# Softmax factors by way of DRAM instead of TensorE, and one load per head instead of one per pair

## The chip, the core and the metric

One core of a Trainium2 chip runs the whole program. Its engines each follow their own list of instructions: TensorE (PE, with its weight loads listed as PEld), VectorE (DVE), ScalarE (ACT), GpSimd (POOL) and SyncE (SP, which only issues DMAs). The metric is the device time in microseconds (us) of one execution; lower is better.

## What is computed

Attention with a mask from hashed buckets, and behind it a gated feed-forward layer. Batch 4, 8 heads, 768 positions, head dimension 64, all in float32:

```
mask   = bucket(q) == bucket(k)            # 6 sign bits of q @ proj, k @ proj
scores = where(mask, q @ k.T / 8, -1e9)    # per batch and head, 768 x 768
attn   = exp(scores - max) / (sum + 1e-9)
x      = attn @ v                          # heads side by side: (4, 768, 512)
h      = relu(x @ w_in)                    # (4, 768, 1024)
out    = (h * sigmoid(conv3(h))) @ w_out
```

## The kernel before

Two heads make a **pair**: 4 pairs for each of 4 batches, 16 in all, named `0_0` to `3_3`. A pair is cut into 12 **units** (6 blocks of 128 queries, 2 heads), and the 192 units run in one loop over `i`; `k` is a unit's place in its pair, 0 to 11. Iteration `i` issues, in this order, the scores `s` of unit `i` (L257, PE), its masked maximum (L270, DVE), the transposes `t` of unit `i-3` (L297, PE) and their copy to SBUF `at` (L304, ACT), and the exponential of unit `i` (L277, ACT), which also leaves the sum of each row. Scores and transposes share a ring of three PSUM tiles (tag `S`), so the scores of a unit reuse the tile of the transposes of two units earlier and wait for their copy.

Every fourth iteration (k = 3, 7, 11; in the text a **burst**) has more: the product with the values `v` (L325, PE) of the last finished group of four units (256 queries, both heads), some steps that decode the float64 weights of the feed-forward layer (L91 to L101 on DVE, a cast L110 on ACT, L111 and L112 on POOL), and a load of raw weights (L132, issued by ACT). How many steps a burst issues stands in `AVS`, `RATE` and `PREP_N`; the order on each engine is just the order in which the code issues.

For the first 7 pairs (not `late`) the division by the sum is done after the product with the values. `Unit.reciprocals` (L291, L292) makes `inv`, 128 queries by 4 (2 blocks by 2 heads), one number per query on the partition of that query. The product `v` has head and dimension on the partitions and queries along the row, so the numbers have to be turned and spread. `spread` (L319) does this on PE, ahead of the 12 chunk products: four products of `inv`, broadcast to 64 columns, with the identity matrix, into the second half of the PSUM tile `av`. `factors` (L330, ACT) copies that to `rs`, and `out` (L333, DVE) multiplies. Later pairs are normalised earlier (L285).

While a pair runs, the next one is prepared: `R` holds queries and keys of both heads (768 KB). `hash` (L186, PE, at k = 3) needs both heads. `split` (head 0 at k = 1 and 3, head 1 at k = 5 and 7) makes on POOL the high part `hi` (L171) and in place the low part (L176), and SP sends these to their places in `Q`, `K`, `q`, `k` (L174, L178). The hash bits go through DVE (L189) and POOL (L191, k = 4) and leave in 8 small DMAs on SP (L195). There is one `R` buffer, so the load for the pair after next (L158, at k = 7) waits until the last low parts have been sent.

Behind pairs 6, 10, 14 and 15 stands a feed-forward stage (`ffn`, L368, L398) of one batch, in which steps of the preparation go on.

All DMAs of the program share eight completion counters, `DMAHW0` to `DMAHW7`, which are given out in turn. A DMA waits on its issuing engine until the one eight before it has landed, whichever engine had issued that one.

Of the kernel before, what the change touches and what calls it, by code (L numbers as in the profile page):

```python
# [7 lines left out]
F32 = mybir.dt.float32  # L8
F32R = mybir.dt.float32r
# [8 lines left out]
P = 128  # L18
# [3 lines left out]
QB = 256  # L22
# [11 lines left out]
AVS = (1 + NCK, 0, 0, 0)  # L34
PREP = 1
PREP_N = 6
# [6 lines left out]
def lsh_attention_conv_ffn(ctx, tc, qk, v, hw, w_in, conv_w, w_out, consts, ident_in, out):  # L43
# [4 lines left out]
    ps = ctx.enter_context(tc.tile_pool(name="ps", bufs=2, space=PSUM))  # L48

# [94 lines left out]
    class Pair:  # L144
        def __init__(self, b, p):
            self.b, self.p, self.nm = b, p, f"{b}_{p}"
            self.late = b * NP + p >= LATE
            self.inv = None

        def load(self):  # L150
            nm = self.nm
            self.R = ring(wp, 1, [P, 2, S], F32R, "R", f"R{nm}")
            src = qk[self.b, 2 * self.p:2 * self.p + 2].rearrange("h p s -> p h s")
            if self.b == self.p == 0:
                for h in range(2):
                    nc.sync.dma_start(self.R[:, h].bitcast(F32), src[:, h])
            else:
                nc.sync.dma_start(self.R.bitcast(F32), src)  # L158
# [8 lines left out]
        def split(self, h):  # L167

            lo, R = self.R[:, h], self.R[:, h].bitcast(F32)
# [6 lines left out]
            nc.gpsimd.tensor_tensor(lo, R, hi.bitcast(F32), ALU.subtract)  # L176
            for dst, src in ((self.Q1[64:, h], lo[:64]), (self.K2[:64, h], lo[64:])):
                nc.sync.dma_start(dst.bitcast(F32), src.bitcast(F32))  # L178

        def hash(self):  # L180
            hp = ring(ps, 3, [P, 2, 512], F32, "S", f"hash{self.nm}")
            R = self.R.bitcast(F32)
            for h in range(2):
                for half in range(2):
                    g = 32 * (2 * h + half)
                    nc.tensor.matmul(hp[g:g + 32, 0, :HS], hw_sb[:, :32], R[:, h, half * HS:(half + 1) * HS],  # L186
                                     start=True, stop=True, tile_position=(0, g))
# [22 lines left out]
        def prepare_now(self):  # L210
# [3 lines left out]
            for h in range(2):  # L214
                hps.append(ring(ps, 2, [P, 512], F32, "M", f"hash{nm}_{h}")[:, :HS])
                for g in range(4):
                    c, half = 32 * (1 + g // 2), g % 2
                    nc.tensor.matmul(hps[h][32 * g:32 * g + 32], hw_sb[:, c:c + 32],
                                     self.R[:, h, half * HS:(half + 1) * HS].bitcast(F32),
                                     start=True, stop=True, tile_position=(0, 32 * g))  # L220
            for h in range(2):
                R = self.R[:, h].bitcast(F32)
# [22 lines left out]
    class Unit:  # L245
# [14 lines left out]
        def maximum(self, prev):  # L260
# [6 lines left out]
            self.sum = self.st[:, 2:3] if pr.late else pr.sums[:, 2 * self.tq + self.h, 0:1]  # L267
# [25 lines left out]

        def transposes(self):
# [12 lines left out]
    def values(pr, qb, ats, inv):  # L307
# [7 lines left out]
        def spread():  # L315

            for t in range(QB // P):
                for h in range(2):
                    nc.tensor.matmul(av[h * D:(h + 1) * D, QB + t * P:QB + (t + 1) * P],  # L319
                                     inv[:, 2 * t + h:2 * t + h + 1].to_broadcast([P, D]), ident,  # L320
                                     start=True, stop=True, tile_position=(0, h * D))

# [5 lines left out]

        def factors():
            nc.scalar.copy(rs, av[:, QB:2 * QB])  # L330
# [18 lines left out]
        rs = ring(wp, 2, [P, QB], F32, "rs", f"rs{pr.nm}_{qb}")  # L349
        return [spread, *chunks], (factors, out, parts)  # L350
# [91 lines left out]
    pairs[0].load()  # L442
# [6 lines left out]
    pairs[1].load()  # L449
    av, outs, lows, early = [], [], [], None  # L450
    n = len(units)
    ffn_after = {min((b + 1) * NP - 1 + DEFER, B * NP - 1): b for b in range(B)}
    for i in range(n + LAG):
# [22 lines left out]
        if two and not two.pair.late and two.tq == QB // P - 1 and two.h == 1:  # L476
            two.reciprocals()
# [20 lines left out]
        for _ in range(1 + NCK if ending else AVS[(i - LAG) % 4]):  # L498
# [20 lines left out]
        if w and w.tq == QB // P - 1 and w.h == 1:  # L519
            if not ending:  # L520
                av.append(values(w.pair, w.qb, w.pair.at, w.pair.inv))
            else:
                def fill():
                    steps, last = values(w.pair, w.qb, w.pair.at, w.pair.inv)
# [56 lines left out]
```

## Time and profile before

| | |
|---|---|
| time, median of 3 runs | 740.08 us (740.05 to 745.73) |
| profiled execution | 739.48 us, its span 737.5 us |
| granted TensorE clock | 0.997 |
| busy: PE, DVE, ACT, POOL | 710.9, 487.3, 498.5, 331.9 us |
| attention of the first 7 pairs | about 0 to 221 us of the span |
| L319 (`spread`) on PE, L330 (`factors`) on ACT | 13.8 us in 168 instructions, 7.8 us in 21 |

The span runs from the first to the last instruction; the execution has 1.98 us around it. A busy time joins overlapping instructions, since matrix products are pipelined: from start to start the next one often comes sooner than the listed length.

### The profile page before, as it was taken

The page shows a single profiled execution, that of the slowest core. Times are in us where ns is not written, and L with a number is a line of the kernel's source. Part 1 is how long each engine was busy: PE and PEld are TensorE (multiplying, and loading weights), DVE is VectorE, ACT ScalarE, POOL GpSimd, SP SyncE. Part 2 cuts the span into 40 slices and gives each one's busy share as a digit, 9 for nine tenths or more (in the row PEclk, how much of TensorE's full clock was granted, in tenths as well). Part 3 has the DMA queues.
Part 4 walks back from the last instruction along what each step waited for, and adds up shares of the span by engine and source line. Part 5 has one row for each costly group of instructions (what it writes and reads, how often), then busy time and mean ns, then how long its engine had stood idle before and what let it go on. Part 6 is the DMA issues. An engine that isn't in the chain of part 4 may idle for free.

```text
span 737.5 us, 13543 instructions
## 1 busy us (share of the span) xinstructions
PE 710.9 (96%) x4720; PEld 589.0 (80%) x4720; DVE 487.3 (66%) x1211; ACT 498.5 (68%) x937; POOL 331.9 (45%) x334
## 2 busy tenths in 40 slices
PE   6998999899899999999999999999999999999997
PEld 3787777678778988777877998778778899878996
DVE  7977878788775755666665666466666566555663
ACT  5788578678684554877877554778778655585554
POOL 4265456357463522475673532355755232241321
PEclk9999999999999999999999999999999999999999
DMA  4867666663552310237545130324463001100011
GB/s 143 222 187 202 165 186 166 165 166 89 147 146 52 86 44 36 72 77 189 139 105 149 34 94 3 108 60 113 117 180 95 1 0 44 44 1 1 0 44 43
DMA packets 30355, 72.17 MB, mean 98 GB/s; under 512 B 5936, under 2 KB 7504, under 8 KB 30288
## 3 DMA queue, kind: packets, MB, share of 16 engines
q1 hardware_dynamic: 27696, 62.88, 32.0%
q10 hardware_dynamic: 2592, 8.44, 3.3%
q8 instruction: 37, 0.61, 0.3%
q14 instruction: 30, 0.25, 0.1%
HBM read 27.40 MB, written 6.29 MB: 46 GB/s over the span
## 4 chain that ended last, share of the span: by engine, by line
PE 69%; DMA 11%; POOL 7%; issue 5%; DVE 4%; SPq 3%; ACT 1%; POOLq 0%; DVEq 0%; ACTq 0%
PE h L368 19%; PE o L398 18%; PE v L325 11%; PE s L257 10%; PE t L297 9%; DMA R<-in_qk 6%; DMA k<-R 4%; POOL R L176 2%; SPq L174 2%; DVE e L270 1%; DMA K<-hi 1%; PE hash L186 1%; POOL hi L171 1%; ACT e L277 1%; SPq L178 1%
## 5 line engine op out<-in xcount | busy, mean ns | idle before, releaser
L270 DVE TENSOR_SCALAR_CACHE_REDUCE e<-s 128x768 f32<-128x768 f32 x192 | 183.2, 954 | 81.2 <-PE s L257 70.6
L277 ACT ACTIVATE e<-e,st 128x768 f32<-128x768 f32 x192 | 181.3, 944 | 10.3 <-DVE st L284 5.0
L304 ACT COPY at<-t 128x768 f32<-128x768 f32 x192 | 152.3, 794 | 47.0 <-PE t L297 47.0
L297 PE MATMUL t<-ident,e 128*128 128x128 f32 x1152 | 160.0, 275 | 3.6 <-POOL e L285 1.5
L377 DVE SCALAR_TENSOR_TENSOR ht<-ht,cw 128x384 f32<-128x384 f32 (+1 forms) x128 | 114.7, 896 | 71.2 <-ACT ht L375 69.0
L387 POOL TENSOR_TENSOR g<-ht,g 128x384 fp32r<-128x384 f32 x64 | 71.5, 1117 | 179.5 <-ACT g L386 141.8
L297 PEld LDWEIGHTS t<-ident,e 128*128 128x128 f32 x1152 | 130.6, 141 | 22.3 <-POOL e L285 7.4
L285 POOL TENSOR_SCALAR e<-e,st 128x768 f32<-128x768 f32 x108 | 98.3, 911 | 103.1 <-DVE st L284 51.4
L398 PE MATMUL o<-wo,g 128*128 128x512 f32 x576 | 142.4, 394 | 0.0
L368 PE MATMUL h<-xh,wi 128*128 128x386 f32 x512 | 141.9, 340 | 0.0
L325 PE MATMUL v<-at,v 128*64 128x256 f32 x1152 | 135.6, 385 | 0.0
L398 PEld LDWEIGHTS o<-wo,g 128*128 128x128 f32 x576 | 107.4, 188 | 20.3
L257 PE MATMUL s<-K,Q 128*128 128x384 f32 x384 | 116.7, 385 | 1.9 <-ACT e L277 1.0
L325 PEld LDWEIGHTS v<-at,v 128*64 128x64 f32 x1152 | 81.2, 138 | 42.4 <-issue 8.6
L257 PE MATMUL s<-k,q 96*128 96x384 f32 x384 | 100.2, 342 | 2.1 <-ACT q L237 1.9
L368 PEld LDWEIGHTS h<-xh,wi 128*128 128x128 f32 x512 | 94.1, 188 | 4.8 <-issue 1.8
L380 ACT ACTIVATE ht<-ht 128x384 f32<-128x384 f32 x64 | 33.6, 526 | 91.4 <-DVE ht L377 91.4
L368 PE MATMUL h<-xl,wi 128*128 128x386 f32 x256 | 86.7, 339 | 0.0
L257 PEld LDWEIGHTS s<-K,Q 128*128 128x128 f32 x384 | 59.0, 192 | 23.2 <-issue 16.6
L257 PEld LDWEIGHTS s<-k,q 96*128 96x128 f32 x384 | 70.7, 191 | 3.5 <-ACT q L237 3.0
L381 DVE TENSOR_TENSOR ht<-ht 128x384 f32<-128x384 f32 x64 | 40.2, 629 | 33.4 <-ACT ht L380 33.4
L176 POOL TENSOR_TENSOR R<-R,hi 128x768 fp32r<-128x768 f32 x30 | 56.6, 1886 | 0.2
(75 smaller groups left out, 586.0 us busy)
## 6 DMA issues: line engine op xcount, KB each, us to landing
R<-in_qk SPq DMA_DIRECT2D x15, 768.0 KB
K<-hi SPq DMA_DIRECT2D x60, 192.0 KB
v<-in_v SPq DMA_DIRECT2D x16, 384.0 KB
out<-osb SPq DMA_DIRECT2D x24, 256.0 KB
Q<-hi SPq DMA_DIRECT2D x30, 192.0 KB
q<-hi SPq DMA_DIRECT2D x30, 192.0 KB
Q<-R SPq DMA_DIRECT2D x30, 192.0 KB
k<-R SPq DMA_DIRECT2D x30, 192.0 KB
```

The source lines that it names most:

```text
L176: nc.gpsimd.tensor_tensor(lo, R, hi.bitcast(F32), ALU.subtract)
L257: nc.tensor.matmul(self.sp[:, half, :HS], A[:, h, qs], C[:, h, half * HS:(half + 1) * HS], start=(kk == 0), stop=(kk == 1))
L270: nc.vector.tensor_scalar(self.e.rearrange("p (a b) -> p a b", a=2), self.sp[:, :, :HS], MASKED, None, ALU.max, ALU.max, accum_out=self.st ...
L277: nc.scalar.activation(self.e, self.e, AF.Exp, bias=self.st[:, 1:2], scale=SCALE, accum_out=self.sum)
L285: nc.gpsimd.tensor_scalar(self.e, self.e, self.st[:, 3:4], 0.0, ALU.mult, ALU.add)
L297: nc.tensor.transpose(self.tp[:, c // 3, c % 3 * P:(c % 3 + 1) * P], self.e[:, c * P:(c + 1) * P], ident)
L304: nc.scalar.copy(pr.at[self.h][:, :, :, self.tq * P:(self.tq + 1) * P], self.tp[:, :, :3 * P].rearrange("p j (c q) -> p j c q", c=3))
L325: nc.tensor.matmul(av[h * D:(h + 1) * D, :QB], vt[:, c, h, :], ats[h][:, c // 3, c % 3, :], start=(c == 0), stop=(c == NCK - 1), tile_posi ...
L368: nc.tensor.matmul(hp[:, :HW], w, x[:, c0:c0 + HW], start=(n == 0), stop=(n == 3 * NCC - 1))
L377: nc.vector.scalar_tensor_tensor(t[:, a:z], ht[:, o + k - 1 + a:o + k - 1 + z], cw[:, f, k:k + 1], t[:, a:z], ALU.mult, ALU.add)
L387: nc.gpsimd.tensor_tensor(g[:, 1, :], t, g[:, 0, :].bitcast(F32), ALU.subtract)
L398: nc.tensor.matmul(op, l, r, start=(f == 0 and n == 0), stop=(f == NFC - 1 and n == 2))
```

## The change

`spread` and `factors` go. In their place `reciprocals` returns three steps for ACT: `write` (L299) sends `inv` to a scratch tile `row` in DRAM, [2 heads, 2 blocks, 128], an iteration later nothing is done, and in the one after that `read` (L303, one DMA per head) fetches each head's 256 numbers into its 64 partitions of `rs`, the same row for each partition. `values` gets `rs` ready made. `R` becomes two tiles, `R0` and `R1`, one for each head, with a load for each: head 0 of the pair after next at k = 4, head 1 at k = 8, ahead of the load of `v`. The sums are stored in another order.

```diff
-AVS = (1 + NCK, 0, 0, 0)
+AVS = (NCK, 0, 0, 0)
-PREP_N = 6
+PREP_N = 3, 7
...
-        def load(self):
+        def load(self, h):
...
+            self.R[h] = ring(wp, 1, [P, S], F32R, f"R{h}", f"R{nm}_{h}")
+            nc.sync.dma_start(self.R[h].bitcast(F32), qk[self.b, 2 * self.p + h])
...
             nc.vector.reciprocal(pr.inv, pr.inv)
+            row = ring(dp, 4, [2, QB // P, P], F32, "row", f"row{self.nm}")
+            rs = pr.rs = ring(wp, 2, [P, QB], F32, "rs", f"rs{self.nm}")
+            def write():
+                nc.scalar.dma_start(row.rearrange("h t q -> q (h t)"), inv)
+            def read():
+                for h in range(2):
+                    nc.scalar.dma_start(rs[h * D:(h + 1) * D],
+                                        row[h].rearrange("t q -> (t q)").unsqueeze(0).to_broadcast([D, QB]))
+            return [write, None, read]
...
-        def spread():
-            for t in range(QB // P):
-                for h in range(2):
-                    nc.tensor.matmul(av[h * D:(h + 1) * D, QB + t * P:QB + (t + 1) * P],
-                                     inv[:, 2 * t + h:2 * t + h + 1].to_broadcast([P, D]), ident,
-                                     start=True, stop=True, tile_position=(0, h * D))
-        def factors():
-            nc.scalar.copy(rs, av[:, QB:2 * QB])
...
-            two.reciprocals()
+            spreads.append(two.reciprocals())
...
+        for steps in spreads:
+            if steps:
+                step = steps.pop(0)
+                if step:
+                    step()
...
-        if u and k == PREP + PREP_N and pi + 1 < len(pairs):
+        if u and k - PREP in PREP_N and pi + 2 < len(pairs):
+            pairs[pi + 2].load(PREP_N.index(k - PREP))
+        if u and k - PREP == PREP_N[1] and pi + 1 < len(pairs):
             pairs[pi + 1].load_v()
-            if pi + 2 < len(pairs):
-                pairs[pi + 2].load()
```

Three places show what the change moves. Line numbers behind L290 are higher with the change (L311 is L297 of before, L318 is L304, L331 is L325, L111 and L133 are L110 and L132), and in rows without buffer numbers the batch is left out of a name as well. The first is PE in the burst at k = 3 of pair `0_3`, in which the hash of pair `1_0` is followed by the last group of pair `0_2`. Before:

```order
L257 MATMUL s_3_1_1_1273<-K_3_720,Q_3_719 128x384 x2
L257 MATMUL s_3_1_1_1273<-k_1_82,q_1_80 128x384 x2
L297 MATMUL t_3_0_0_1282<-ident,e_3_0_0_1214 128x128 x6
L186 MATMUL hash_0_1294<-R_0_1089,hw_sb 32x384 x4
L319 MATMUL v_2_2_1271<-ident,inv_2_5_1_1235 64x128 x4
L325 MATMUL v_2_2_1271<-at_2_2_0_1171,v_2_715 64x256
```

With the change:

```order
L257 MATMUL s_3_1_1_1278<-K_3_744,Q_3_743 128x384 x2
L257 MATMUL s_3_1_1_1278<-k_1_84,q_1_82 128x384 x2
L311 MATMUL t_3_0_0_1287<-ident,e_3_0_0_1217 128x128 x6
L186 MATMUL hash_0_1301<-R_0_0_988,hw_sb 32x384 x2
L186 MATMUL hash_0_1301<-R_0_1_1112,hw_sb 32x384 x2
L331 MATMUL v_2_2_1277<-at_2_2_0_1177,v_2_745 64x256
```

The four products of L319 are gone, and the hash reads two tiles. The second place is ACT from the exponential of k = 5 of pair `0_3` on. Before, up to the copy of k = 8, with what each row waits for:

```order
L277 ACTIVATE e0_3_3_0_1368,sums1_74<-e0_3_3_0_1368,st0_3_3_0_1367 128x768 [waits DVE_49,Activation_49]
L304 COPY at0_3_0_1_1290<-t0_3_1_1_1398 128x6x128 [waits PE_49]
L277 ACTIVATE e0_3_2_1_1395,sums1_74<-e0_3_2_1_1395,st0_3_2_1_1394 128x768 [waits DVE_49,Activation_49]
L304 COPY at0_3_1_0_1427<-t0_3_2_0_1420 128x6x128 [waits PE_49]
L277 ACTIVATE e0_3_3_1_1417,sums1_74<-e0_3_3_1_1417,st0_3_3_1_1416 128x768 [waits DVE_49,Activation_49]
L110 CAST wi3_1_1453<-upi3_1_1325 128x512 [waits DMAHW3_49,DVE_49]
L132 DMA rawo4_1471<-in_w_out 128x1024 [waits DMAHW5_49]
L330 COPY rs0_3_0_1410<-v0_3_0_1409 128x256 [waits PE_49,Pool_49]
L304 COPY at0_3_1_0_1427<-t0_3_3_0_1483 128x6x128 [waits PE_49]
```

With the change:

```order
L277 ACTIVATE e0_3_3_0_1372,sums1_76<-e0_3_3_0_1372,st0_3_3_0_1371 128x768 [waits DVE_49,Activation_49]
L299 DMA row0_3_1_1_1378<-inv0_3_1_1_1375 128x4x1 [waits DVE_49]
L318 COPY at0_3_0_1_1295<-t0_3_1_1_1405 128x6x128 [waits PE_49]
L277 ACTIVATE e0_3_2_1_1402,sums1_76<-e0_3_2_1_1402,st0_3_2_1_1401 128x768 [waits DVE_49,Activation_49]
L318 COPY at0_3_1_0_1433<-t0_3_2_0_1426 128x6x128 [waits PE_49]
L277 ACTIVATE e0_3_3_1_1423,sums1_76<-e0_3_3_1_1423,st0_3_3_1_1422 128x768 [waits DVE_49,Activation_49]
L303 DMA rs0_3_1_1_1379<-row0_3_1_1_1378 64x256 [waits DMAHW4_49,DMAHW3_49,Pool_49]
L303 DMA rs0_3_1_1_1379<-row0_3_1_1_1378 64x256 [waits DMAHW5_49]
L111 CAST wi3_1_1457<-upi3_1_1328 128x512 [waits DVE_49]
L133 DMA rawo4_1469<-in_w_out 128x1024 [waits DMAHW7_49]
L318 COPY at0_3_1_0_1433<-t0_3_3_0_1480 128x6x128 [waits PE_49]
```

A write stands behind the exponential of k = 5 and two reads behind that of k = 7, ahead of the cast; the copy L330 is gone. The counters `DMAHW3` and `DMAHW5` for which the two reads wait belong, by the turn, to the first two bits DMAs (L195) of the same iterations. The third place is SP, from the last bits DMA of pair `0_3` (k = 4 of pair `0_2`) to the first part of pair `1_0` (k = 1 of pair `0_3`). Before:

```order
L195 DMA q_1_80<-bits_3_928 12x384
L174 DMA Q_3_719<-hi_3_1_1006 64x768
L174 DMA q_1_80<-hi_3_1_1006 64x768
L174 DMA K_3_720<-hi_3_1_1006 64x768 x2
L178 DMA Q_3_719<-R_3_717 64x768
L178 DMA k_1_82<-R_3_717 64x768
L165 DMA v_3_1087<-in_v 128x768
L158 DMA R_0_1089<-in_qk 128x2x768
L174 DMA Q_0_1091<-hi_0_0_1247 64x768
```

With the change:

```order
L195 DMA q_1_82<-bits_3_936 12x384
L156 DMA R_0_0_988<-in_qk 128x768
L174 DMA Q_3_743<-hi_3_1_1014 64x768
L174 DMA q_1_82<-hi_3_1_1014 64x768
L174 DMA K_3_744<-hi_3_1_1014 64x768 x2
L178 DMA Q_3_743<-R_3_1_741 64x768
L178 DMA k_1_84<-R_3_1_741 64x768
L156 DMA R_0_1_1112<-in_qk 128x768
L165 DMA v_3_1116<-in_v 128x768
L174 DMA Q_0_1114<-hi_0_0_1253 64x768
```

The load of head 0 moves ahead of head 1's high parts, and that of head 1 ahead of `v`.

More of the change, by code (lines that the diff above doesn't have):

```diff
@@ L146, in __init__ @@
             self.b, self.p, self.nm = b, p, f"{b}_{p}"
+            self.R = [None, None]
             self.late = b * NP + p >= LATE
-            self.inv = None
-        def load(self):
+            self.inv = self.rs = None
+        def load(self, h):
             nm = self.nm
-            self.R = ring(wp, 1, [P, 2, S], F32R, "R", f"R{nm}")
-            src = qk[self.b, 2 * self.p:2 * self.p + 2].rearrange("h p s -> p h s")
-            if self.b == self.p == 0:
-                for h in range(2):
-                    nc.sync.dma_start(self.R[:, h].bitcast(F32), src[:, h])
-            else:
-                nc.sync.dma_start(self.R.bitcast(F32), src)
+            self.R[h] = ring(wp, 1, [P, S], F32R, f"R{h}", f"R{nm}_{h}")
+            nc.sync.dma_start(self.R[h].bitcast(F32), qk[self.b, 2 * self.p + h])
+            if h == 0:
+                return
             self.Q1 = ring(wp, 2, [P, 2, S], F32R, "Q1", f"Q1{nm}")
@@ L181, in hash @@
             hp = ring(ps, 3, [P, 2, 512], F32, "S", f"hash{self.nm}")
-            R = self.R.bitcast(F32)
             for h in range(2):
+                R = self.R[h].bitcast(F32)
                 for half in range(2):
                     g = 32 * (2 * h + half)
-                    nc.tensor.matmul(hp[g:g + 32, 0, :HS], hw_sb[:, :32], R[:, h, half * HS:(half + 1) * HS],
+                    nc.tensor.matmul(hp[g:g + 32, 0, :HS], hw_sb[:, :32], R[:, half * HS:(half + 1) * HS],
                                      start=True, stop=True, tile_position=(0, g))
@@ L266, in maximum @@
             self.sums = None if pr.late else pr.sums
-            self.sum = self.st[:, 2:3] if pr.late else pr.sums[:, 2 * self.tq + self.h, 0:1]
+            self.sum = self.st[:, 2:3] if pr.late else pr.sums[:, 2 * self.h + self.tq, 0:1]
             e = wp.tile([P, 776], F32, tag="e", name=f"e{self.nm}", bufs=EB)
@@ L292, in reciprocals @@
             nc.vector.reciprocal(pr.inv, pr.inv)
+            inv = pr.inv
+            row = ring(dp, 4, [2, QB // P, P], F32, "row", f"row{self.nm}")
[7 more added lines that the diff above has]
+            return [write, None, read]
         def transposes(self):
@@ L305, in to_sbuf, with values @@
                            self.tp[:, :, :3 * P].rearrange("p j (c q) -> p j c q", c=3))
-    def values(pr, qb, ats, inv):
+    def values(pr, qb, ats, rs):
         if qb == 0:
@@ L348, in values @@
             return chunks, (out_high, out_low, lambda: None)
-        rs = ring(wp, 2, [P, QB], F32, "rs", f"rs{pr.nm}_{qb}")
-        return [spread, *chunks], (factors, out, parts)
+        return chunks, (lambda: None, out, parts)
     g2, prep = [None], [iter(()), iter(())]
@@ L441, in lsh_attention_conv_ffn @@
              for t in range(qb * QB // P, (qb + 1) * QB // P)]
-    pairs[0].load()
+    for h in range(2):
+        pairs[0].load(h)
     nc.sync.dma_start(ident, ident_in)
@@ L448, in lsh_attention_conv_ffn @@
     next(first)
-    pairs[1].load()
-    av, outs, lows, early = [], [], [], None
+    for h in range(2):
+        pairs[1].load(h)
+    av, outs, lows, early, spreads = [], [], [], None, []
     n = len(units)
@@ L497, in lsh_attention_conv_ffn @@
             prepare(0)
-        for _ in range(1 + NCK if ending else AVS[(i - LAG) % 4]):
+        for _ in range(NCK if ending else AVS[(i - LAG) % 4]):
             if av:
@@ L520, in lsh_attention_conv_ffn @@
             if not ending:
-                av.append(values(w.pair, w.qb, w.pair.at, w.pair.inv))
+                av.append(values(w.pair, w.qb, w.pair.at, w.pair.rs))
             else:
+                for steps in spreads:
+                    while steps:
+                        step = steps.pop(0)
+                        if step:
+                            step()
                 def fill():
-                    steps, last = values(w.pair, w.qb, w.pair.at, w.pair.inv)
+                    steps, last = values(w.pair, w.qb, w.pair.at, w.pair.rs)
                     for step in [*steps, *last]:
```

8 lines of the change are left out of this document (4 added, 4 removed).

## Prediction

> **What bounds the kernel now.** I read the totals first, then the busy time of each engine (PE, PEld, DVE, ACT, POOL, in that order) in the two parts of the span, before and after the first feed-forward stage begins.
>
> ```profile
> PE 710.9 (96%) x4720; PEld 589.0 (80%) x4720; DVE 487.3 (66%) x1211; ACT 498.5 (68%) x937; POOL 331.9 (45%) x334
> ```
>
> ```profile
> 0.00:221.00 221.00, 202.98 (x1573) 160.20 (x1573) 179.49 (x448) 164.88 (x304) 114.81 (x123) 0.99 0.60 166
> 221.00:737.00 516.00, 507.90 (x3151) 428.82 (x3148) 307.85 (x763) 333.60 (x634) 217.05 (x212) 1.00 0.25 69
> ```
>
> PE bounds the program, but not evenly. Behind 221 us it lacks 8 us of 516. In the first 221 us, where nearly all that the change touches lies, it lacks 18, DVE is busy for 81% of the time and ACT for 75%: three engines are close together there. The waits of PE tell what it lacks, and the groups what the removed lines cost.
>
> ```profile
> PE hash L186 <- DMA R<-in_qk: 9.1, 9, 2.2
> ```
>
> ```profile
> L319 PE MATMUL v<-ident,inv 128*64 128x128 f32 x168 | 13.8, 285 | 0.0
> L330 ACT COPY rs<-v 128x256 f32<-128x256 f32 x21 | 7.8, 371 | 18.2 <-PE v L325 15.6 <-PE t L297 1.3 <-DMA rawi<-in_w_in 1.2
> ```
>
> The columns of the wait are us in total, times, longest: the hash that stands nine times for the load of `R` is the largest single wait of PE. Now PE's own rows at one burst, and the first and the last hash of six whole pairs.
>
> ```profile
> 43.35 0.85 PE L186 MATMUL hash<-R,hw_sb 128*32 128x384 f32 x8
> ...
> 103.10 0.85 PE L186 MATMUL hash<-R,hw_sb 128*32 128x384 f32 x8 [0.49 <-DMA R<-in_qk]
> 103.89 0.66 PE L319 MATMUL v<-ident,inv 128*64 128x128 f32 x8
> 104.37 2.76 PE L325 MATMUL v<-at,v 128*64 128x256 f32 x24
> 107.06 0.61 PE L257 MATMUL s<-K,Q 128*128 128x384 f32 x2
> ...
> 108.44 0.59 PE L257 MATMUL s<-K,Q 128*128 128x384 f32 x2
> ...
> 220.17 0.85 PE L186 MATMUL hash<-R,hw_sb 128*32 128x384 f32 x8 [1.48 <-DMA R<-in_qk]
> ```
>
> From start to start a hash takes 0.79 us, `spread` 0.48, the products with `v` 2.69, a unit 1.38. A pair so asks PE for 12 x 1.38 + 3 x (0.48 + 2.69) + 0.79 = 26.9 us. It gets one in (220.17 - 43.35) / 6 = 29.5 us. Without `spread` PE would need 25.4.
>
> The last view is the preparation chain of pair `1_1` on POOL and SP, with the chain that ended last behind it, and what PE waits for there.
>
> ```profile
> 112.81 0.58 POOL L191 TENSOR_SCALAR bits<-bits,cst 128x384 fp32r<-128x384 f32 x1
> ...
> 121.38 1.82 POOL L176 TENSOR_TENSOR R<-R,hi 128x768 fp32r<-128x768 f32 x1
> ```
>
> ```profile
> 114.89 0.76 SPq L195 DMA_DIRECT2D q<-bits  x1
> ...
> 119.63 0.71 SPq L195 DMA_DIRECT2D q<-bits  x1
> ...
> 125.22 0.54 SPq L165 DMA_DIRECT2D v<-in_v  x1
> ```
>
> ```profile
> 0.74 3.38 DMA R<-in_qk
> ...
> 94.39 2.96 DMA k<-R
> ...
> 123.76 5.43 DMA k<-R
> 129.24 4.32 DMA R<-in_qk
> 136.47 1.95 DMA K<-hi
> ```
>
> ```profile
> 118.74 0.60 PE L257 MATMUL s<-K,Q 128*128 128x384 f32 x2
> ...
> 128.85 0.59 PE L257 MATMUL s<-K,Q 128*128 128x384 f32 x2 [1.01 <-ACT e L277]
> ...
> 133.70 0.85 PE L186 MATMUL hash<-R,hw_sb 128*32 128x384 f32 x8 [1.82 <-DMA R<-in_qk]
> ```
>
> The low part of head 1 ends on POOL at 123.2, its transfers at 129.2, only then the 768 KB load of `R` starts, and the hash runs when that has landed. The scores at 128.85, the first of head 1, are late by the same transfers.
>
> **The change part by part.**
>
> *`spread` off PE.* Three bursts a pair, 7 pairs: 21 x 0.48 = **10.1 us** (the 13.8 us of the group overlap their neighbours). All of it is PE's own time.
>
> *`factors` off ACT.* ACT stood 18.2 us before these 21 copies, mostly for PE: no gain by itself. DVE, POOL and the number of units stay as they are; the sums' new order and the shorter `AVS` cost nothing, since the instructions that use them are the same.
>
> *`R` by heads.* Head 0 is loaded one iteration after its low part, and POOL's first `hi` need not wait for it any more. Head 1 still goes after the transfers of its own low part, but with half the bytes, and `v` goes behind it. A 384 KB load took 3.38 us here (0.74, with its twin in flight), against 4.32: 0.94 less. The transfer of `k` took 5.43 us in the place where `v` was issued into it, 2.96 at 94.39: some 1.5 less. Against that PE comes earlier: of a pair's three spreads one (0.48) lies between the burst that triggers the last low part and the hash. So 2.4 - 0.5 = 1.9 us go from each wait, and the longest was 2.2. I leave 0.3 for each of 7 and book 9.1 - 2.1 = **7.0 us**. The extra DMA issues on SP (16, at some 0.4 us) lie where SP waits anyway.
>
> *Write and reads on ACT.* ACT gets three DMAs for each group of four units. Their bounds and their place are the risk of this change.
>
> ```profile
> 111.03 0.94 ACT L277 ACTIVATE e<-e,st 128x768 f32<-128x768 f32 x1
> ...
> 111.96 0.79 ACT L304 COPY at<-t 128x768 f32<-128x768 f32 x1
> ...
> 114.25 0.95 ACT L277 ACTIVATE e<-e,st 128x768 f32<-128x768 f32 x1
> 115.09 0.20 ACT L277 ACTIVATION_READ_ACCUMULATOR e<-e,st 128x1 f32 x1
> 116.88 0.62 ACT L110 CAST wi<-upi 128x512 fp32r<-128x512 f32 x1 [1.59 <-DVE lowi L101]
> 116.95 0.33 ACTq L132 DMA_DIRECT2D rawo<-in_w_out  x1
> ...
> 117.67 0.80 ACT L304 COPY at<-t 128x768 f32<-128x768 f32 x1
> ```
>
> An issue takes 0.33 us (ACT's own, above) to 0.76 us (SP's, of 12 rows), and it overlaps what ACT is executing: the one at 116.95 lies under the cast of 116.88. The write follows the exponential of 111.03 and has 0.9 us until the copy of 111.96. The reads follow the one of 114.25, where ACT then idles 1.59 us until the cast: 0.7 to 1.5 us of issue fit. Behind the reads stand that cast (POOL's next decode step and, behind it, the last low part wait for it) and the copy of 117.67, for which the scores at 118.74 wait.
>
> Two things can hold the reads. One is the write's landing. The trace has no store of 4-byte pieces. The nearest row is the last store of the output:
>
> ```profile
> SPq L577 <- DMA out<-osb: 1.9, 1, 1.9
> ```
>
> SP waited 1.9 us for that one, so landing takes about 2.2 with the issue. From the write at about 111.1 to the reads' place at 114.3 are 3.2 us, and with 1.6 of idle time less the two issues about 4 us cost nothing. For the pieces themselves the queue gives the bound from above:
>
> ```profile
> q1 hardware_dynamic: 27696, 62.88, 32.0%
> ```
>
> 32% of 16 queues over 737.5 us for 27696 packets are 136 ns for one of 2.3 KB in the mean; 512 pieces on 16 engines at that price last 4.4 us, at nothing 0. So the landing is between 2.2 and 6.6 us; I take 3 to 4, nearer to the first, because the pieces are 4 bytes and not 2.3 KB, and so nothing. At 6.6 the reads would be late by 2.6 us.
>
> The Trainium skill, "DMA: Bandwidth & Descriptors", section "Rules for kernel authors", speaks against this write: a transfer whose last dimension is not contiguous becomes one descriptor for each element, and it advises to rearrange it. Its section "Specifications" adds that pieces under 512 B cost a read-modify-write. No run here shows the price yet; by these sentences the landing would lie toward the upper end and the sum toward the second rival.
>
> The other is the turn of the eight counters. In pairs `0_1`, `0_3` and `1_1` the two reads at k = 7 wait for the first bits DMAs of that preparation. In `0_3` the second of these was issued at 114.89; with a landing of at least 1.95 (the row at 136.47) that is 116.84, when ACT has been free since 115.3. With the two issues, cast and copy come about 1 us later than before, while PE is 0.96 earlier by two spreads: the scores of 118.74 stand up to 1.6 us. In the other pairs the bits went out sooner, since no decode step of POOL preceded them. I take 1.2 us for three pairs, **-3.5 us**; the ends are 0 and 6 x 1.6 = 10.
>
> **Sum.** 10.1 + 7.0 - 3.5 = 13.6 us. The profiled execution took 739.5 us (737.5 of span and 2 around it), 0.6 below the median of 740.08: 739.5 - 13.6 = **726 us**, a pair in some 27.3 us instead of 29.5.
>
> **Rivals.**
>
> *DVE and the preparation take PE's place; the gain is small.* DVE has 179 us of work in what would be some 207 us (87%), and it decodes in long runs just when PE does the products with `v`, which now begin 0.48 us sooner. For it: in the first part all engines but POOL are above 74%. Against it: 28 us of slack, and PE may run ahead by a unit. If PE keeps only half of the spreads (5) and the waits for `R` come back by half (4.5) while the counters cost 3.5, the gain is 6 us: **733**.
>
> *ACT is held in front of the reads; slower.* One mechanism, the landing of the write: it decides from about 4 us on, when the reads come after the place of the cast. Each us above that delays cast, copies and scores in each of 21 groups. At the bound of 6.6 us it is 2.6 x 21 = 55 us against 17 of gain, at 5.5 us 32: between **754** and 777, of which I take the near end. For it: 4-byte stores, two transfers in a row before anything can go on, ACT in order. Against it: 1.95 to 2.2 us for landings here.
>
> *The load by heads does nothing.* The hash needs both heads, and head 1 still starts after the same transfers. Then only 10.1 - 3.5 = 6.6 are left: 733, as in the first rival, to which I add it.
>
> **Chances and range.** Forecast (719 to 731) 0.62; everything removed is kept, with the 1.0 us at 128.85 and some more, 717, 0.04; the two rivals about 733 0.18; slower 0.16. One per cent, about what a measurement of this kernel can tell from no change, is 7.4 us: faster (below 732) gets the forecast, the best case and a little of the rivals at 733, 0.68; within 0.17, slower 0.15. The range has to leave out no more than 0.2: from **717** (all gains, no cost) to **741**, which takes in the rivals at 733 with the counters at their upper end and leaves the held ACT out.
>
> **What would show it.** PE's rows without L319, and the step from hash to `v` 0.8 us. The wait of PE's hash for `R` at 2 us or less in total, not 9. The low parts of head 1 landing within 4 us of their issue. ACT's reads issued before or just behind the cast's old place, with idle time of ACT in front of them in three pairs. A DVE busy share near 87% in the first part. The forecast is wrong if ACT's copies (L304 before) stand behind a read for more than 1.6 us in most groups, which would show as PE's scores waiting for ACT, or if hashes still come every 29 us though PE has no L319.

## The result, and the profile after

| | before | with the change |
|---|---|---|
| time, median | 740.07 us (739.51 to 745.73) | 836.44 us (831.86 to 843.35) |
| ratio | | 1.129, 95% interval 1.124 to 1.134 |
| profiled execution, its span | 739.48 us, 737.5 us | 839.82 us, 838.0 us |
| start of the first feed-forward stage on PE | 220.95 us | 313.96 us |

The kernel became 96 us slower where 14 us of gain were forecast. First the totals of the changed kernel:

```profile
PE 740.5 (88%) x4552; PEld 608.7 (73%) x4552; DVE 490.7 (59%) x1211; ACT 493.7 (59%) x916; POOL 331.1 (40%) x334
```

Its busy time ahead of and behind the start of the first feed-forward stage, with the granted clock, the queues' share and their GB/s as the last three columns:

```profile
0.00:314.00 314.00, 228.95 (x1413) 178.28 (x1413) 182.84 (x448) 160.03 (x282) 114.75 (x123) 0.85 0.62 125
314.00:838.00 524.00, 511.55 (x3144) 430.40 (x3140) 307.84 (x763) 333.70 (x635) 216.38 (x212) 0.99 0.26 68
```

93 of some 100 us lie in the first part. There PE's idle time went from 18 us (221 - 202.98) to 85 us (314 - 228.95), and PE was busy 26 us longer although the 13 us of L319 in this part are gone: the rest of its work took some 39 us more, at a mean granted clock of 0.85 instead of 0.99. The sum, 67 + 39 - 13, is the 93.

What PE waits for in the changed kernel (us in total, times, longest):

```profile
PE s L257 <- ACT at L318: 53.2, 17, 6.1
PE hash L186 <- DMA R<-in_qk: 9.4, 2, 8.2
```

And its timeline from one write on, rows of ACT, POOL and PE:

```profile
116.91 0.38 ACTq L299 DMA_DIRECT2D row<-inv  x1
...
126.04 1.10 ACTq L303 DMA_DIRECT2D rs<-row  x2
...
127.18 0.62 ACT L111 CAST wi<-upi 128x512 fp32r<-128x512 f32 x1 [6.50 <-DMA k<-bits]
...
127.85 0.80 ACT L318 COPY at<-t 128x768 f32<-128x768 f32 x1
127.88 1.27 POOL L112 TENSOR_TENSOR upi<-upi,wi 128x512 f32<-128x512 f32 x1 [13.88 <-ACT wi L111]
...
128.70 1.01 PE L257 MATMUL s<-K,Q 128*128 128x384 f32 x2 [4.79 <-ACT at L318]
```

The write is issued at 116.91 and the reads only at 126.04, 9.1 us later; cast and copy stand behind them, and PE stands 4.79 us for the copy. The product behind that pause takes 1.01 us for two, 0.61 in before, and the trace lists the granted clock at a half there. A landing is told in what follows by the completion counter: from the start of the issue to the last rise of the counter before the next transfer takes it. By this the 21 writes landed after 8.1 to 12.0 us, 9.1 in the median; the one of 116.91 at 125.97, just ahead of the reads. The chain that ended last holds them as well, with start and length:

```profile
86.69 12.02 DMA row<-inv
102.05 6.37 DMA row<-inv
...
285.62 8.92 DMA row<-inv
296.15 8.57 DMA row<-inv
```

Read like this, the picture is that of the second rival: ACT held in front of the reads. The first experiments were made to see whether that was the loss.

### The profile page after: what moved, and what is told of

It reads as the page before. It is cut to its first block, busy times and chain, and to the rows that moved or that the text cites. A ratio compares the mean times of both kernels' runs of the same rounds, so it can differ in the third digit from the quotient of the medians.

```text
span 838.0 us, 13359 instructions
## 1 busy us (share of the span) xinstructions
PE 740.5 (88%) x4552; PEld 608.7 (73%) x4552; DVE 490.7 (59%) x1211; ACT 493.7 (59%) x916; POOL 331.1 (40%) x334
## 3 DMA queue, kind: packets, MB, share of 16 engines
q10 hardware_dynamic: 17040, 11.24, 7.0%
## 4 chain that ended last, share of the span: by engine, by line
PE 60%; DMA 20%; issue 8%; POOL 5%; ACT 3%; DVE 2%; ACTq 1%; SPq 1%; POOLq 0%; DVEq 0%
PE h L370 16%; PE o L400 16%; PE v L331 9%; PE s L257 9%; PE t L311 8%; DMA row<-inv 8%; DMA k<-R 2%; DMA R<-in_qk 2%; DMA rawi<-in_w_in 2%; POOL R L176 1%; ACT e L277 1%; DMA q<-hi 1%; DMA k<-bits 1%; ACTq L303 1%; DMA v<-in_v 1%
## 5 line engine op out<-in xcount | busy, mean ns | idle before, releaser
L318 ACT COPY at<-t 128x768 f32<-128x768 f32 x192 | 152.3, 794 | 79.4 <-PE t L311 47.6
L311 PE MATMUL t<-ident,e 128*128 128x128 f32 x1152 | 173.1, 290 | 7.9 <-DVE e L270 5.9
L257 PE MATMUL s<-K,Q 128*128 128x384 f32 x384 | 125.3, 410 | 58.8 <-ACT at L318 53.2
L311 PEld LDWEIGHTS t<-ident,e 128*128 128x128 f32 x1152 | 143.4, 150 | 27.5 <-DVE e L270 7.9
L370 PE MATMUL h<-xh,wi 128*128 128x386 f32 x512 | 143.7, 344 | 4.6 <-ACT ht L375 4.6
L331 PE MATMUL v<-at,v 128*64 128x256 f32 x1152 | 140.8, 392 | 5.3 <-ACT at L318 5.2
L257 PEld LDWEIGHTS s<-K,Q 128*128 128x128 f32 x384 | 63.8, 207 | 84.6 <-ACT at L318 62.5
L331 PEld LDWEIGHTS v<-at,v 128*64 128x64 f32 x1152 | 82.6, 140 | 56.7 <-issue 18.1
L257 PE MATMUL s<-k,q 96*128 96x384 f32 x384 | 106.0, 359 | 2.4 <-ACT q L237 2.4
L370 PEld LDWEIGHTS h<-xh,wi 128*128 128x128 f32 x512 | 95.6, 191 | 10.1 <-ACT ht L375 5.1
L257 PEld LDWEIGHTS s<-k,q 96*128 96x128 f32 x384 | 76.6, 206 | 3.3 <-ACT q L237 3.2
```

The source lines that it names most:

```text
L257: nc.tensor.matmul(self.sp[:, half, :HS], A[:, h, qs], C[:, h, half * HS:(half + 1) * HS], start=(kk == 0), stop=(kk == 1))
L311: nc.tensor.transpose(self.tp[:, c // 3, c % 3 * P:(c % 3 + 1) * P], self.e[:, c * P:(c + 1) * P], ident)
L318: nc.scalar.copy(pr.at[self.h][:, :, :, self.tq * P:(self.tq + 1) * P], self.tp[:, :, :3 * P].rearrange("p j (c q) -> p j c q", c=3))
L331: nc.tensor.matmul(av[h * D:(h + 1) * D, :QB], vt[:, c, h, :], ats[h][:, c // 3, c % 3, :], start=(c == 0), stop=(c == NCK - 1), tile_posi ...
L370: nc.tensor.matmul(hp[:, :HW], w, x[:, c0:c0 + HW], start=(n == 0), stop=(n == 3 * NCC - 1))
```

## Experiments

Ratios are to the kernel before, on the same chip. Line numbers of each kernel differ by a few.

### Is it ACT's wait in front of the reads?

The reads three iterations later:

```diff
-            return [write, None, read]
+            return [write, None, None, None, None, read]
...
```

> As the changed kernel, but with the two reads issued three iterations later (four empty steps between write and reads, not one), some 11 us behind the write. Theory 1 (ACT stands in front of the reads until the write has landed, 8 to 9 us, and with it copies, casts and scores): the wait is gone, 720 to 740. Theory 2 (the eight counters' turn: ACT waits for SP's transfers): the same transfers are in the turn, 790 or more. Theory 3 (512 small pieces a group slow the other transfers, and so the preparation): the pieces stay, 800 or more.

Measured: 901.07 us, ratio 1.214 (1.208 to 1.220). Theory 1 in that form fell: with the reads out of the way the kernel is slower still. Where the time went stands in the groups of this run, at the multiplication (busy us, mean ns, then idle time in front of it):

```profile
L336 DVE TENSOR_TENSOR rs<-v,rs 128x256 f32<-128x256 f32 x21 | 8.9, 425 | 131.4 <-DMA rs<-row 131.2
```

The reads were now issued just behind the write of the next group, and landed 6 to 8 us later with it; DVE stood 131 us for them. A transfer that has nothing to do with a write comes late when it is issued beside one.

The reads from another tensor, so that nothing waits for the write:

```diff
-  row[h].rearrange("t q -> (t q)").unsqueeze(0).to_broadcast([D, QB]))
+  qk[pr.b, 2 * pr.p + h, 0:1, :QB].to_broadcast([D, QB]))
```

> As the changed kernel, write and reads at the same places, but the reads fetch the same number of bytes from the query and key tensor in DRAM, so that they need not wait for the write; the factors are therefore other numbers than the sums' reciprocals. Theory 1 (waiting for the write's landing): 720 to 740. Theory 2 (counters' turn): the turn is the same, about 836. Theory 3 (traffic of the small pieces): about 836.

Measured: 852.51 us, 1.151 (1.143 to 1.160): no gain at all. Its timeline around one write, the issues of SP and ACT:

```profile
116.00 0.90 SPq L195 DMA_DIRECT2D k<-bits  x1
116.39 0.39 ACTq L299 DMA_DIRECT2D row<-inv  x1
...
118.23 0.51 ACTq L303 DMA_DIRECT2D rs<-in_qk  x1
...
119.73 6.89 SPq L174 DMA_DIRECT2D K<-hi  x2
125.98 0.47 ACTq L303 DMA_DIRECT2D rs<-in_qk  x1
```

The bits DMA of 116.00, 18 KB and issued even before the write, landed at 125.96 by its counter, after 9.96 us; the one issued ahead of it took 2.76. The second read has the same counter and so stands until 125.98, and SP's issue of `K` stands 6 us in the same manner. ACT is held at its old place, but by a transfer that the write holds up, through the turn of the counters.

### The write by itself

The kernel before, with the write added and nothing else; no one reads it:

```diff
+        def write(self):
+            row = ring(dp, 4, [QB // P, 2, P], F32, "row", f"row{self.nm}")
+            nc.scalar.dma_start(row.rearrange("t h q -> q (t h)"), self.pair.inv)
```

> The kernel before with nothing but the write of the changed kernel added, at the same place on ACT, 512 pieces of 4 bytes to 2 KB of scratch that nothing reads; spread, its copy and the single load of R stay. If the small stores alone hold up all transfers and that is the loss: 815 to 845, landing 8 us or more. If it takes the reads' wait for the write on ACT as well: 745 to 770.

Measured: 831.77 us, 1.121 (1.115 to 1.127). That is 89 of the 96 us, with no read, no wait on ACT for one, and `spread` in its place. Here the waits of PE have another name:

```profile
PE hash L187 <- DMA R<-in_qk: 51.7, 9, 9.3
PE s L258 <- ACT at L309: 11.1, 4, 3.4
PE s L258 <- DMA Q<-R: 8.1, 3, 5.7
```

The timeline around one write, with the load of `R` on SP ahead of it and the hash on PE behind it:

```profile
45.60 0.39 SPq L159 DMA_DIRECT2D R<-in_qk  x1
...
47.35 0.38 ACTq L297 DMA_DIRECT2D row<-inv  x1
...
55.11 1.51 PE L187 MATMUL hash<-R,hw_sb 128*32 128x384 f32 x8 [5.95 <-DMA R<-in_qk]
```

Busy times of the stretch in between, with the queues' GB/s as the last column:

```profile
50.50:56.00 5.50, 0.89 (x8) 0.23 (x8) 0.00 (x0) 1.13 (x3) 0.83 (x1) 0.83 0.02 2
```

And that load in the chain that ended last, with its length:

```profile
45.60 9.37 DMA R<-in_qk
```

The load of 768 KB, issued 1.75 us ahead of the write, took 9.37 us, and the six behind it 8.3 to 11.2, where those of before took 4.1 to 6.0 in this part. The 2 GB/s from 50.5 to 56 us are no measure of what the queues could carry: the load's packets were all under way by 50.7, and SP issued nothing more until 55.91. What came late were the rises of the load's counter, the last five of 16 at 54.45 to 54.97, and the write's own, the last at 56.56. Where more is under way, it is slowed as well. In the changed kernel the load of one head of `R` and two transfers of high parts were issued from 120.45 to 121.59, and the queues (last column) moved 34 GB/s, against 166 in the first part of before:

```profile
118.50:125.00 6.50, 5.41 (x42) 4.07 (x38) 4.90 (x13) 2.18 (x5) 0.00 (x0) 1.00 0.48 34
```

Of the packets of 3 KB in the first part of this run, 275 of 8704 took over 1 us, up to 7.1; in before 11 did, up to 1.1. So 2 KB in 512 pieces hold up what is on the queues beside them until they have landed themselves. What then waits is decided by what happens to be under way: here `R`, in the changed kernel the bits and the reads. The first theory is wrong about the place, the third right.

### What makes the write so slow

Four numbers together, 128 pieces of 16 bytes:

```diff
-                nc.scalar.dma_start(row.rearrange("h t q -> q (h t)"), inv)
+                nc.scalar.dma_start(row.rearrange("h t (q k) -> (h t q) k", k=4), inv)
```

> As the changed kernel, but the write keeps each partition's four numbers together: 128 pieces of 16 bytes instead of 512 of 4 bytes. The reads fetch the same rows of the scratch, so the factors stand in another order than the queries. If the landing grows with the number of pieces (8 to 9 us for 512 would be about 2 to 4 for 128): 725 to 755. If a store to DRAM with a read behind it has a landing of its own, whatever the pieces: 820 to 840. Theory 2 (counters) expects about 836 as well.

Measured: 768.32 us, 1.035 (1.028 to 1.041); landing in 1.4 to 7.0 us, median 2.7. The bulk of the loss is gone. Two things changed with it, the number of pieces and their size, so 512 pieces were put apart (reads from the other tensor as in the run of 852 us):

```diff
-            row = ring(dp, 4, [2, QB // P, P], F32, "row", f"row{self.nm}")
+            row = ring(dp, 4, [2, QB // P, P, 128], F32, "row", f"row{self.nm}")
-                nc.scalar.dma_start(row.rearrange("h t q -> q (h t)"), inv)
+                nc.scalar.dma_start(row[:, :, :, 0].rearrange("h t q -> q (h t)"), inv)
```

> As the kernel whose reads fetch from the query and key tensor (852 us), but each of the 512 numbers of 4 bytes goes to a stretch of 512 bytes of its own in the scratch; the factors are other numbers than the sums' reciprocals. If every small store costs the memory the same wherever it goes: 840 to 865, landing 8 to 9 us. If it is the many stores into one stretch that wait for each other: landing 2 to 3 us and 735 to 760.

Measured: 765.20 us, 1.030 (1.025 to 1.035), landing median 2.5 us. With 16 in place of 128, so that the numbers lie 64 bytes apart:

> As the kernel whose reads fetch from the query and key tensor (852 us), with each number of 4 bytes 64 bytes from the next in the scratch (at 512 bytes it took 765 us and landed in 1.7 to 6.4 us). If stores wait for each other only within 64 bytes: 760 to 770, with the same landing. If the stretch is 512 bytes, with 8 numbers in each: landing 4 to 6 us, 785 to 820.

Measured: 761.47 us, 1.025 (1.022 to 1.029), landing median 2.3 us. With the same 512 pieces of 4 bytes from the same partitions to DRAM the kernel takes 852 us when they lie side by side, and 761 us when they lie 64 bytes apart. So neither their number nor their size alone costs it: 4-byte stores that lie side by side hold each other up, and the other transfers with them. At which distance between 4 and 64 bytes this ends wasn't tried, and how the memory does it isn't seen in the trace. Nor is the write free when its pieces lie apart: the ratio is 1.025 here and 1.011 in the run without any write (below).

To a row of one partition in SBUF instead of DRAM:

```diff
+            row = Q2w[0][96:97].rearrange("o a s -> o (a s)")[:, 512 * r0:512 * (r0 + 1)].bitcast(F32)
+            row = row.rearrange("o (h t q) -> o h t q", h=2, t=2)
...
+                for g in range(4):
+                    nc.scalar.dma_start(row[:, g // 2, g % 2], inv[:, g:g + 1])
```

> As the kernel whose reads fetch from the query and key tensor (852 us), but the same 512 pieces of 4 bytes go to a row on one partition of SBUF, in four transfers of 128, not to DRAM; the factors are other numbers than the sums' reciprocals. If the number of pieces is the cost: 840 to 870. If storing small pieces to DRAM is the cost: landing 2 to 3 us, and 735 to 755 (with 1.2 us more of issues on ACT a group).

Measured: 794.60 us, 1.072 (1.065 to 1.079). The landings are short, a median of 2.7 us, so neighbours of 4 bytes in SBUF, 128 to a transfer, don't hold each other up as in DRAM; but the time lies between the two expectations, and PE waits for ACT's copies, now with the products with `v`:

```profile
PE v L334 <- ACT at L321: 35.9, 14, 6.7
```

Four transfers for one on ACT are a cost of their own, which this run doesn't separate: on the time it is inconclusive.

The clean way through DRAM, 4 pieces of 512 bytes after a transpose on PE, with one load of `R` as in before:

```diff
+            def turn(tp):
+                nc.tensor.transpose(tp[:2 * QB // P, 0, 3 * P:], inv, ident)
+                nc.scalar.copy(itr, tp[:2 * QB // P, 0, 3 * P:])
...
+                nc.scalar.dma_start(row.rearrange("h t q -> (h t) q"), itr)
```

> A candidate: one R and one load as before the change, and the way through DRAM with 4 pieces of 512 bytes: inv is transposed on PE to 4 rows of 128 (one small product instead of four), copied by ACT and written as it stands, and read two iterations later as in the changed kernel. Theory 3 (small stores hold up all transfers): nothing is held up, PE loses 21 x 0.48 us of spread and gains some 21 x 0.15, 730 to 738. If any store with a read behind it costs the way through DRAM: 770 or more. If PE's time in this part is given back to the preparation whatever is taken off it, as the loads by heads alone suggest: 738 to 742.

Measured: 763.02 us, 1.026 (1.022 to 1.031): a miss by 25 us, though the writes landed after 2.4 us in the median. DVE waited for the reads six times:

```profile
DVE rs L346 <- DMA rs<-row: 15.2, 6, 6.6
```

and PE behind ACT and DVE:

```profile
PE s L259 <- ACT at L328: 12.3, 8, 3.2
PE t L321 <- DVE e L272: 11.8, 8, 4.3
```

So two further questions: what do the reads cost, and where is the gain of `spread`?

### The reads alone

No write, reads from the other tensor:

```diff
-            return [write, None, read]
+            return [None, None, read]
...
```

> As the kernel whose reads fetch from the query and key tensor (852 us), and the write is left out too: spread is gone, two reads a group remain, the factors are other numbers than the sums' reciprocals. Theory 3 (the 512 stores of 4 bytes hold up every transfer issued within some 8 us of them): all of the loss goes, 725 to 742. Theory 2 (the counters' turn, in which the reads still stand): 790 or more. The prediction's sum without its 3.5 us for the counters and with the write free would be 722; the run of the loads by heads alone, which gave nothing, speaks for 730 to 738.

Measured: 750.15 us, 1.011 (1.005 to 1.016). All but 8 us of the loss is gone, and the gain isn't there either. One read for both heads in place of two:

```diff
-                for h in range(2):
-                    nc.scalar.dma_start(rs[h * D:(h + 1) * D],
-                                        qk[pr.b, 2 * pr.p + h, 0:1, :QB].to_broadcast([D, QB]))
+                nc.scalar.dma_start(rs, qk[pr.b, 2 * pr.p:2 * pr.p + 2, 0:1, :QB].to_broadcast([2, D, QB]))
```

> As the kernel without the write and with reads from the query and key tensor (750 us), but with one read for each group that fetches both heads' rows, not two. If the reads cost by what they wait for on ACT (the counters' turn, in which each DMA waits for the one eight before it), half of the waits go and with them half of the 10 us to 20 us that the reads cost: 740 to 746. If they cost by their bytes in the queues: 748 to 754.

Measured: 775.49 us, 1.042 (1.039 to 1.046). Both theories missed, on the far side. ACT's queue (packets, MB, share) with two reads:

```profile
q10 hardware_dynamic: 5952, 11.20, 5.5%
```

and with one:

```profile
q10 hardware_dynamic: 5322, 11.19, 5.8%
```

630 packets fewer with all but the same bytes are 30 for each of 21 groups. The Trainium skill, "DMA: Bandwidth & Descriptors", section "Rules for kernel authors", states that a transfer whose outermost dimension is smaller than 16 is confined to so many DMA engines; the outermost here is 2. The packets agree if each engine that takes part ends with one packet: 2 x 16 = 32 before and 2 now. So do the counters: each of the two reads raised its counter 16 times, the one read 3 times, and it landed after 6.9 us in the median (up to 13.5) instead of 3.5. That 64 KB on one engine then hold up the others' shares is argued, not shown; PE's scores waited 16.8 us for low parts of `Q` in this run (2.1 with two reads).

### Where the gain went

The loads by heads alone (`spread`, `factors` and everything else as before):

```diff
-PREP_N = 6
+PREP_N = 3, 7
...
+            self.R[h] = ring(wp, 1, [P, S], F32R, f"R{h}", f"R{nm}_{h}")
+            nc.sync.dma_start(self.R[h].bitcast(F32), qk[self.b, 2 * self.p + h])
```

> The loads by heads alone: spread and factors stay on PE and ACT as before the change, nothing goes through DRAM. The prediction's own term for this part is 7.0 us (9.1 us of the hash's waits for R, 2.1 left), so it expects about 733, and the hash's wait for R at 2 us or less. Rival (the load by heads does nothing, since the hash needs both heads and head 1 still starts after the same transfers): 738 to 740, with the wait near 9 us. If the split itself is what costs the changed kernel its 96 us: above 780.

Measured: 744.84 us, 1.0039 (1.0015 to 1.0063): 3 us slower. The hash's wait for `R` fell as the prediction had said, and other waits of PE took much of its place:

```profile
PE s L256 <- DMA Q<-R: 5.2, 3, 2.2
...
PE s L256 <- DMA k<-R: 1.7, 3, 1.1
...
PE hash L185 <- DMA R<-in_qk: 0.8, 2, 0.6
```

The scores of the next pair now stand for the low parts of `Q` and `k`, among whose transfers the load of head 0 has been put. This isn't the whole, though. In the first part PE idled even a little less than before, 15.9 us against 18.0, and was busy 4.7 us longer with the same work:

```profile
0.00:223.60 223.60, 207.72 (x1572) 162.11 (x1572) 178.49 (x448) 165.11 (x303) 114.38 (x123) 0.98 0.62 164
```

A stretch at half the clock of 6.8 us instead of 3.4 accounts for at most 1.7 of these; the rest stays open.

The changed kernel without any way of the factors, then the same with one `R`:

```diff
-            nc.vector.tensor_tensor(rs, av[:, :QB], rs, ALU.mult)
+            nc.vector.tensor_tensor(rs, av[:, :QB], cst[:, 3:4].to_broadcast([P, QB]), ALU.mult)
...
-            return [write, None, read]
+            return []
```

> As the changed kernel, with loads by heads, but with no way of the factors at all: neither spread and its copy nor write and reads; the multiplication behind the product with v takes a constant in place of the reciprocals. If what is taken off PE is worth what the prediction booked (10.1 us of spread, 7.0 of waits for R): 721 to 727. If the loads by heads give nothing, as measured, and only spread counts: 729 to 733. If PE's time in this part is given back to other waits whatever is taken off it: 738 to 744. What lies between this and the 750 us of the kernel with the reads alone is the price of the two reads on ACT.

Measured: 746.76 us, 1.0046 (1.0020 to 1.0071).

> As the run before it, without any way of the factors and with a constant in their place, but with one R and one load for each pair as before the change. By the prediction's terms 7.0 us more than the run before it, so 728 to 734; if the loads by heads give nothing, equal to it within 2 us.

Measured: 743.17 us, 1.0004 (0.9986 to 1.0021). With `spread` and its copy simply gone, 13.8 us of PE's instructions, nothing changes. The busy times of its first part:

```profile
0.00:222.90 222.90, 195.55 (x1413) 157.69 (x1413) 180.32 (x448) 160.05 (x285) 115.33 (x123) 0.98 0.60 164
```

and its wait for `R`:

```profile
PE hash L187 <- DMA R<-in_qk: 11.8, 7, 3.0
```

PE worked 7.4 us less than before and idled 27.4 us instead of 18: it arrives earlier and waits longer, for `R` 11.8 instead of 9.1. Its busy time fell by only half of the 13.8, at a clock of 0.98 instead of 0.99.

Every product of `spread` issued twice:

```diff
-            for t in range(QB // P):
+            for t in 2 * list(range(QB // P)):
```

> The kernel before with every product of spread issued twice, 8 instead of 4 for each group, the same numbers into the same place. If PE's time at this place costs the program time, as the prediction took it: 750 (10.1 us more). If it lies in time that PE would have waited anyway: 739 to 743.

Measured: 744.88 us, 1.0034 (1.0012 to 1.0057): 2.5 us (0.9 to 4.2) for what was priced at 10.1. PE's time at this place is worth about a quarter of its length when added, and nothing that these runs can tell when removed.

Two buffers for `R`. To make room for the second, the low part of the attention's output overwrites its high part, so the feed-forward stage works on other numbers and one POOL instruction writes in place:

```diff
-            self.R = ring(wp, 1, [P, 2, S], F32R, "R", f"R{nm}")
+            self.R = ring(wp, 2, [P, 2, S], F32R, "R", f"R{nm}")
...
-            pr.x = [ring(wp, NP + DEFER, [P, S], F32R, f"x{k}", f"x{k}{pr.nm}")
-                    for k in "hl"]
+            pr.x = [ring(wp, NP + DEFER, [P, S], F32R, "xh", f"xh{pr.nm}")] * 2
```

> The kernel before with two buffers for R, so that the load no longer waits for the low parts' transfers; to make room, the low part of the attention's output overwrites its high part, so the feed-forward stage gets other numbers, and one POOL instruction writes in place. If the single buffer of R bounds the first part: the 9.1 us of the hash's waits go, 728 to 733. If PE's waits only move: 737 to 742.

Measured: 733.25 us, 0.988 (0.985 to 0.990). Now the 9.1 us are a gain; what is left of that wait:

```profile
PE hash L186 <- DMA R<-in_qk: 3.1, 3, 1.6
```

Two buffers, and no way of the factors:

> Two buffers for R as in the run before, and no way of the factors: spread and its copy are gone and the multiplication takes a constant, as in the run that gave 743. If the single buffer of R took back what spread had given: 717 to 726. If it is something else (DVE at 81% of the first part, copies and decoding steps on ACT): 732 to 743.

Measured: 734.57 us, 0.989 (0.986 to 0.992): `spread` is worth nothing here either, and with it gone the wait for `R` is partly back:

```profile
PE hash L187 <- DMA R<-in_qk: 7.5, 4, 2.8
```

Three of the six DVE instructions that decode each block left out as well:

> As the kernel with two buffers for R and no way of the factors (734.6 us), and of the six DVE instructions that decode each block of weights the second, third and fifth are left out, some 27 us of DVE's 180 in the first part; the weights are therefore other numbers. If DVE is what PE runs into once R and spread are gone: 722 to 728. If it is not: 732 to 736, and the rest stays open.

Measured: 734.31 us, 0.987 (0.983 to 0.992). DVE had 25 us less to do (153.91 of 215 us) and the time did not move, so DVE's work isn't what takes the place. The hash's wait for `R` was 3.4 us in this run, and that did not move the time either. What takes the place stays open.

A version that is complete and has both loads free, three tiles of half a pair in one ring, with the hash bits in the ring of the decoding steps to make room:

```diff
+            self.R[h] = ring(wp, 3, [P, S], F32R, "R", f"R{nm}_{h}")
...
-            bits = ring(wp, 1, [P, HS], F32R, "bits", f"bits{self.nm}")
+            bits = ring(wp, 4, [P, WC], I32, "w", f"bits{self.nm}").bitcast(F32R)[:, :HS]
```

> The kernel before, complete, with R as a ring of three tiles of one head each, so that both loads of the pair after next are issued at the old place and find their tiles free; the hash bits share the ring of the decoding steps to make room. If the wait for R is all that two buffers removed: 732 to 735, the hash's waits for R at 3 us or less. If the load by heads moves the wait to the scores, as the loads by heads alone did: 740 to 745.

Measured: 735.88 us, 0.989 (0.986 to 0.993), the hash's waits at 1.6 us:

```profile
PE hash L185 <- DMA R<-in_qk: 1.6, 2, 1.0
```

This beats the kernel before by 7 us, one per cent, and the changed one by far.

## Why the prediction was wrong

**The step that failed** is the term for the write: "between 2.2 and 6.6 us; I take 3 to 4 [...] and so nothing". Two things in it are wrong. The size: the write landed in 9.1 us (the median of 21, none under 8.1), above its upper bound of 6.6. That bound priced 512 pieces by the packets' times on the queue, but the trace gives each 4-byte packet some 9 ns, and in the median 5.6 us pass behind the last of them (0.5 where they lie 64 bytes apart), where no packet of the write shows them. And the place: the term asked only who waits for this transfer. What it costs is the other transfers: with nobody waiting for the write itself, 89 us.

**The second rival** had the landing as the cause, and PE waiting for ACT's copies as its sign, and both came. But its price, 754 to 777, took ACT's wait as the whole; the reads that didn't wait for the write gave 852, and the write without reads 832.

**The rules of the Trainium skill** that the prediction weighed spoke for the slower side, and direction and count were right: ACT's queue has 14448 packets more than before (17040 against 2592), which is 21 x (512 + 2 x 64 + 3 x 16): one for each number of the write, one for each row of the two reads, and 16 at the end of each of the three transfers. What they say of pieces under 512 B doesn't give the price, though: 512 such pieces landed in 2.3 us when they lay 64 bytes apart.

**Spread off PE, 10.1 us:** measured 0 (1.0004), and 2.5 us for doubling it. The prediction saw PE at 203 of 221 us and took every us there for the program's. By its own rows PE waited each pair for `R`, and work ahead of a wait is covered by it. It allowed for this with one of a pair's three spreads; all three were covered: without them PE was busy 7.4 us less, at a slightly lower clock, and idled 9.3 us more.

**R by heads, 7.0 us:** in the run of the loads alone the wait fell from 9.1 to 0.8 us, as forecast, and the time rose by 3 us. The step counted the bytes in front of the hash but not the other users of the same queues: the scores that wait for the low parts took 6.9 us, and PE's work took 4.7 us more, for the most part from a cause that stays open. Two buffers, which take the load out of the cycle instead of moving it, gave 9.2 us, and 7.0 in the complete version.

**The counters' turn, 3.5 us:** the reads cost about 4.5 us (1.0106 against 1.0046; with both intervals, 0 to 9). The size agrees, loosely; that the turn is what costs them wasn't put to a run. Of the signs, the hash followed by `v` and L319 gone came. The others failed: PE's wait for `R` is 9.4 us; the low parts of head 1 for `Q` landed after 5.2 to 8.3 us, not 4; DVE's share is 58% (182.84 of 314), not 87%.

By measured terms: 740 + 0 (spread) + 3 (loads) + 4.5 (reads) + 88 (write, 1.1288 against 1.0106) = 836. The last term is what the run without the write leaves, so the sum closes by itself; the check on it is the write alone, with 89.

## What to carry to other kernels

Price a small store by what it does to the queues, not by its bytes or its packets: look at how long the transfers beside it take to land, against the same transfers without it. Lay 4-byte pieces 64 bytes apart, or make them contiguous before they leave. Then ask whether the way through DRAM pays at all: none of those tried here came under 761 us. A busy engine that has a wait in every round can give nothing back when work ahead of the wait goes; test a term by doubling and by removing it before believing in either, and take a wait away by a second buffer rather than by an earlier load into the same one.

## What the runs showed of the hardware

- 512 stores of 4 bytes side by side to 2 KB of DRAM landed in 9.1 us, the median of 21, and transfers beside them came late, also one issued ahead of the store: loads of 768 KB took 8.3 to 11.2 us instead of 4.1 to 6.0. 64 or 512 bytes apart the stores landed in 2.3 and 2.5 us, 128 pieces of 16 bytes side by side in 2.7, and 4-byte pieces in SBUF, 128 to a transfer, in 2.7.
- PE's clock fell to half in stretches of 3.4, 6.8 or 10.2 us: 19 in the first 330 us of the changed kernel, 1 in the first part of before. They came with the pauses and lasted into the work behind them, some 39 us of longer work beside 67 us more of waiting. The Trainium skill, "TensorE: Matmul & The Clock Gate", section "What's actually happening", names a window of about 3.4 us and half clock after an idle one; the lengths agree.
- A kernel with one read in place of two, for the same bytes and with an outermost dimension of 2, took 25 us longer; the read landed after 6.9 us instead of 3.5.
